# First attention tile scored in two halves, three weight conversions moved in VectorE's order, some high parts on VectorE

## The chip, the cores and the metric

The kernel runs on one core of a Trainium2 chip. The metric is the device time of one execution in microseconds; several runs are taken and their median is given. Engines are named as the profile names them: PE is the matrix engine (TensorE), PEld its weight loads, DVE is VectorE, ACT is ScalarE, POOL is GpSimd and SP is SyncE, which here only issues transfers. Every engine works through its own instructions in the order in which the program issues them, and waits where an instruction needs something that is not there yet.

## The reference

Two stages. First, attention over 8 batches, 8 heads, 576 positions and 64 channels a head, with a causal window of 64 positions. Then a mixer over the attention's output, first across positions (tokens), then across channels, each with a residual or sum:

```
scores = q @ k.T / 8;  masked unless 0 <= pos_q - pos_k < 64
attn   = softmax(scores);   x = attn @ v                 # x: (8, 576, 512)
h = relu(x.T @ w_tok1) @ w_tok2;  u = x + h.T            # 576 -> 256 -> 576
out = u + relu(u @ w_ch1) @ w_ch2                        # 512 -> 1536 -> 512
```

q, k and v are 32-bit floats; the four weight matrices arrive as 64-bit floats, and the kernel turns them into 32-bit floats itself by integer operations.

## The kernel before, in words

Products of the mixer are made exact enough by splitting each factor into a rounded high part (`hi`) and the rest (`lo`) and adding three matmuls, hi by hi, hi by lo and lo by hi. So almost every tile goes through a rounding copy (mostly ScalarE) and a subtraction (VectorE or GpSimd); `split` (L107) does both.

The attention and the token mixer run in one loop (L483) over i from -1 to 36. There are 36 attention tiles: `tile_blocks` (L81) gives each two blocks of 64 queries, nine tiles for a pair of batches. The loop is pipelined by hand; a pass i holds, in the order in which instructions are issued:

- loads of v for tile i+2, q for tile i+3, and k for a batch (L484 to 489), all on SyncE's queue;
- `pt_transpose` (L308) of tile i: PE transposes eight blocks of exponentials (pp), ScalarE copies them out (pt, L314);
- `softmax` (L285) of tile i+1: eight VectorE operations (L297) that add the mask, scale and take the minimum of the negated scores, one for each head;
- `recip` (L329) of the sums of tile i; in passes before `N_START` = 7 its first step is on GpSimd (L333), later on VectorE (L335);
- `job_finish` (L253) of a converted weight: high part on ScalarE, low part on GpSimd or, for the token mixer's second matrix, on VectorE (both L109 and L112);
- `split_x` (L346) of an attended tile that is ready: xhi on ScalarE, xlo on GpSimd (L109, L112);
- `softmax_exp` (L300) of tile i+1: eight exponentials on ScalarE (L305), four for u = 0 and four for u = 1, where u is the odd or even head of a pair;
- `tok1` (L443) of an earlier tile: six matmuls into h (L372); at the last tile of a batch `finish_h` (L379) takes the two high parts hhi from h on ScalarE (L383), and `finish_h_low` (L386) the low parts hlo on VectorE (L392);
- `av` (L319): 32 matmul records of attended values, xp (L324), and `norm` (L339), VectorE's multiplication by the reciprocal sums (L341);
- `qk` (L269) of tile i+2: 32 matmul records of scores, s (L282);
- `tok2` pieces (L400): transposes and matmuls into up (L413, L420), copied to u by ScalarE (L425); `run_pieces` is called after the first exponentials and again at the end of a pass. The bank that up lies in is single, so a piece waits until the copy of the piece before it is done.

Weight conversions are jobs, at most one a pass, by the hand-written table `JOBS` (L43); jobs 0 to 3 belong to w_tok1, jobs 4 to 6 to w_tok2. A job has a first half, `job_convert_a` (VectorE, L204, L206, L207), a second half, `job_convert_b` (VectorE, L216, L218, L219, then GpSimd's addition w, L221), and `job_finish` in the next pass. Before pass 7 both halves stand behind `norm`; from pass 7 on the first half stands ahead of `tok1` and the second behind the exponentials and ahead of `av` and `norm`. Passes 7 and 8 convert jobs 5 and 6.

`qk(0)` puts its scores into two banks of the tag "s" (u = 0 and 1, four heads each), `qk(1)` into the two of the tag "h", later tiles into "s". Banks of one tag are reused in turn, and the reuse waits for the last reader. xp lies in the single bank "av".

Ahead of the loop (L462 to 473) SyncE's queue issues the first loads in this order: q of tile 0; the first two blocks of k of the two groups that tile 0 needs, in one transfer; q of tile 1; the rest of these groups' blocks; v of tile 0; the first raw weights; the last k blocks; q of tile 2; raw weights; v of tile 1. Five matmuls on zeros (L480, L481, ten records) stand ahead of `qk(0)`.

The second stage, the channel mixer (from L562), follows; the change does not touch it.

Of the kernel before, what the change touches and what calls it, by code (L numbers as in the profile page):

```python
# [10 lines left out]
F32 = mybir.dt.float32  # L11
# [4 lines left out]
AF = mybir.ActivationFunctionType  # L16
# [28 lines left out]

TOK1_FROM, TOK1_SLOW, TOK2_FROM = 2, 7, 9

N_START = 7

NX = 4  # L50
NCHUNK = TOK // CHUNK
# [39 lines left out]
def mixer_kernel(ctx: ExitStack, tc: tile.TileContext, qh, kh, vh, wt1, wt2, wc1, wc2, out):  # L91
# [39 lines left out]
    with ExitStack() as actx:  # L131
# [16 lines left out]
        def load_q(i):  # L148
            qr = pq.tile([P, H // 2, 2, BLK], F32, name=f"q{i}", tag="q", bufs=5)
            nc.sync.dma_start(qr, qh[i])  # L150
            loaded[i] = [qr, None]
# [94 lines left out]
        def job_convert_b():  # L246
            if to_convert_b:
                n, part = to_convert_b.pop(0)
                to_finish.append((n, to_f32_b(*part)))
# [19 lines left out]
        def qk(i):  # L269

            qt = loaded[i][0]
            s = []
            for u in range(2):

                s.append(ps.tile([P, 4, P], F32, name=f"s{i}_{u}", tag="h" if i == 1 else "s", bufs=2))
                s_ps[i, u] = s[u]
            for j in range(4):
                for u in range(2):
                    r = slice(u * BLK, (u + 1) * BLK)
                    for half, (b, n) in enumerate(tile_blocks(i)):  # L280
                        so = s[u][half * BLK:(half + 1) * BLK, j].rearrange("p (n c) -> p n c", n=2)
                        nc.tensor.matmul(so, qt[r, j, half], kbs[b][r, n:n + 2, j],  # L282
                                         start=True, stop=True)

        def softmax(i, u):  # L285
            if u == 0:
                st[i] = (pa.tile([P, H], F32, name=f"nm{i}", tag="nm", bufs=3),
                         pa.tile([P, H], F32, name=f"sum{i}", tag="sum", bufs=3))
            nm, sm = st[i]
            mk = mask[1 if tile_blocks(i)[0][1] == 0 else 0]  # L290
            e = pa.tile([P, 4, P], F32, name=f"e{i}_{u}", tag="e", bufs=4)
            e_sb[i, u] = e

            s = s_ps.pop((i, u))
            for h in range(4):
                g = 2 * h + u
                nc.vector.tensor_tensor_reduce(out=e[:, h], in0=s[:, h], in1=mk, scale=-scale, scalar=MAX_F32,  # L297
                                               op0=ALU.add, op1=ALU.min, accum_out=nm[:, g:g + 1])

        def softmax_exp(i, u):  # L300
            e = e_sb[i, u]
            nm, sm = st[i]
            for h in range(4):
                g = 2 * h + u
                nc.scalar.activation(e[:, h], e[:, h], AF.Exp, bias=nm[:, g:g + 1], scale=-1.0,  # L305
                                     accum_out=sm[:, g:g + 1])

# [71 lines left out]
        def finish_h(b):  # L379
            h_hi[b] = []  # L380
            for tt in range(NTT):
                hi = pa.tile([P, C], F32R, name=f"hhi{b}_{tt}", tag=f"hhi{tt}", bufs=2)
                nc.scalar.activation(hi, h_ps[b][tt], AF.Relu)  # L383
                h_hi[b].append(hi)

        def finish_h_low():  # L386
# [71 lines left out]
        def run_pieces(k):  # L458
            for _ in range(min(k, len(pieces))):
                tok2(*pieces.pop(0))  # L460

        load_k(0)  # L462
        load_q(0)
        k0, kh0 = (x[:, :8].rearrange("p (g n) j c -> p g n (j c)", g=2) for x in (kbs[0], kh[0]))
        nc.sync.dma_start(k0[:, :, :2], kh0[:, :, :2])
        load_q(1)
        nc.sync.dma_start(k0[:, :, 2:], kh0[:, :, 2:])
        load_v(0)
        job_load()
        nc.sync.dma_start(kbs[0][:, 8:], kh[0, :, 8:])  # L470
# [12 lines left out]
        for i in range(-1, NT + 1):  # L483
            if 0 <= i and i + 2 < NT:  # L484
                load_v(i + 2)
            if 3 <= i + 3 < NT:
                load_q(i + 3)
            if i + 4 < NT:
                load_k(i + 4)
            store_u()  # L490
            n_jobs = JOBS[i]
            if i == NT - 1:
                up_tags += [("s", 2), ("pt", 2)]
            have = len(pieces)
            n_pieces = PIECES.get(i, (1, 1) if i >= TOK2_FROM else (0, 0))
            pts = []
            if 0 <= i < NT:
                pts.append(pt_transpose(i, 0))
                if i < NT - 1:
                    pts.append(pt_transpose(i, 1))  # L500
            if i + 1 < NT:
                softmax(i + 1, 0)
            if i + 1 < NT:
                softmax(i + 1, 1)
            if 0 <= i < NT:
                ri = recip(i)
            if i >= N_START:
                while to_finish:
                    job_finish()
            for n in tok1_plan.get(i + 1, ()):  # L510
                last_use = n - NX + ((n - NX) % TPP == 4)
                if n < i and last_use not in tok1_plan.get(i, ()):
                    split_x(n)
            while to_finish:
                job_finish()
            if i + 1 < NT:
                softmax_exp(i + 1, 0)
            run_pieces(min(have, n_pieces[0]))
            have = min(have, len(pieces))
            if i >= N_START:  # L520
                for _ in range(n_jobs):
                    job_convert_a()
            if i == NT - 1:
                pts.append(pt_transpose(i, 1))
            if i < N_START:
                softmax_exp(i + 1, 1)
            for n in tok1_plan.get(i, ()):
                tok1(n)
            if N_START <= i < NT - 1:
                softmax_exp(i + 1, 1)  # L530
            if i >= N_START:
                for _ in range(n_jobs):
                    job_convert_b()
            if 0 <= i < NT:
                norm(i, av(i, pts), ri)
            finish_h_low()
            if i < N_START:
                for _ in range(n_jobs):
                    job_convert_a()
                    job_convert_b()  # L540
            if i + 2 < NT:
                qk(i + 2)
            for n in tok1_plan.get(i + 1, ()):
                if n not in xhl:
                    split_x(n)
            run_pieces(min(have, n_pieces[1]))
            while to_load and len(to_convert) < 2 and i < NT - 2:
                job_load()
            if i == NT - 1:
                while to_convert or to_convert_b or to_finish:  # L550
                    job_convert_a()
                    job_convert_b()
                    job_finish()
                qctx.close()
                pu = uctx.enter_context(tc.tile_pool(name="pu", bufs=1, side="right", reuse_waits="tile"))
                ul = {0: load_u(0, pu)}
# [537 lines left out]
```

## Time and profile before

| what | value |
|---|---|
| median of 3 runs | 800.99 us (800.95 to 801.45) |
| the profiled execution | 801.79 us, its span 799.8 us |
| PE busy | 787.4 us, 98% of the span |
| VectorE busy | 570.2 us, 71% |
| ScalarE busy | 388.3 us, 49% |
| GpSimd busy | 262.5 us, 33% |
| granted PE clock | 0.999 |
| traffic | 180.59 MB, mean 226 GB/s |

Times in the profile count from the start of the span. A row of a timeline gives the start, the duration, the engine, the line, the operation, the output and inputs by the program's names, and in brackets how long the engine had been idle before and what ended that. Rows that follow one another may be merged, with their count at the end.

### The profile page before, as it was taken

Reading aid. Unit: us, or ns where it says so; the run is one execution under the profiler, and the core shown is the slowest. Engines: PE = TensorE matmul, PEld = TensorE weight load, DVE = VectorE, ACT = ScalarE, POOL = GpSimd, SP = SyncE. Lnnn points to the kernel's source line nnn. Section 1 sums busy time; section 2 is a strip of 40 time slices with the busy share of each in tenths; the row PEclk is TensorE's granted clock in tenths of the full one; section 3 lists DMA queues with packets and bytes.
Section 4 is the critical chain, followed back from the end, with each engine's and each line's share of the span. In section 5 each row is a group of like instructions: output and inputs, shape, how many; then the busy total and the mean of one; then the engine's idle time right before and its main releaser. Section 6 shows DMA issues by size and latency. Waiting matters only on the chain.

```text
span 799.8 us, 15811 instructions
## 1 busy us (share of the span) xinstructions
PE 787.4 (98%) x5749; PEld 654.8 (82%) x5749; DVE 570.2 (71%) x1533; ACT 388.3 (49%) x1124; POOL 262.5 (33%) x237
## 2 busy tenths in 40 slices
PE   8999999999999999999999999999999999999997
PEld 6667888888889888888888888888888888888886
DVE  5978789589582795777788474757766667656576
ACT  6999889889874441323334141326332244324040
POOL 3634545445330000000000050549732638723140
PEclk9999999999999999999999999999999999999999
DMA  9856779668635537877655775765985756955543
GB/s 352 282 179 229 235 251 304 223 217 308 218 113 170 197 103 216 257 225 235 207 164 193 275 289 184 258 236 203 294 320 201 288 187 207 349 209 191 201 159 105
DMA packets 86828, 180.59 MB, mean 226 GB/s; under 512 B 8800, under 2 KB 51808, under 8 KB 84832
## 3 DMA queue, kind: packets, MB, share of 16 engines
q1 hardware_dynamic: 84640, 177.76, 64.4%
q10 hardware_dynamic: 2112, 1.84, 0.7%
q8 instruction: 45, 0.74, 0.4%
q14 instruction: 31, 0.25, 0.1%
HBM read 137.69 MB, written 41.88 MB: 225 GB/s over the span
## 4 chain that ended last, share of the span: by engine, by line
PE 93%; ACT 3%; DVE 3%; POOL 1%; issue 1%; DVEq 0%; ACTq 0%
PE op L969 22%; PE gp L913 21%; PE op L643 12%; PE gp L635 12%; PE up L420 6%; PE h L372 6%; PE xp L324 4%; PE s L282 3%; PE pp L312 3%; PE up L413 3%; ACT e L305 2%; DVE e L297 1%; PE idle L481 1%; DVE x L341 1%; POOL xlo L112 0%
## 5 line engine op out<-in xcount | busy, mean ns | idle before, releaser
L913 PE MATMUL gp<-m,w1hi 128*128 128x512 f32 x504 | 155.1, 389 | 0.0
L112 POOL TENSOR_TENSOR m7lo<-t3g,m7hi 128x512 fp32r<-128x512 f32 x18 | 23.4, 1300 | 359.4 <-ACT m7hi L109 359.4
L305 ACT ACTIVATE e<-e,nm 128x128 f32<-128x128 f32 x288 | 112.3, 398 | 5.7 <-DVE nm L297 5.7
L913 PEld LDWEIGHTS gp<-m,w1hi 128*128 128x128 f32 x504 | 94.6, 188 | 19.6
L913 PE MATMUL gp<-m,w1lo 128*128 128x512 f32 x252 | 98.0, 389 | 0.0
L958 DVE TENSOR_TENSOR uf<-op,uf 128x512 f32<-128x512 f32 (+1 forms) x91 | 61.9, 684 | 39.5 <-PE op L969 31.7
L297 DVE CUSTOM_DVE_ANT_0 e<-s,mask 128x128 f32<-128x128 f32 x288 | 63.5, 286 | 12.5 <-PE s L282 12.4
L112 POOL TENSOR_TENSOR xlo<-x,xhi 128x512 fp32r<-128x512 f32 x32 | 41.2, 1289 | 46.3 <-ACT xhi L109 46.0
L305 ACT ACTIVATION_READ_ACCUMULATOR e<-e,nm 128x1 f32 x288 | 56.3, 196 | 0.0
L635 PE MATMUL gp<-ulo,w1hi 128*128 128x512 f32 x144 | 56.0, 389 | 0.0
L635 PE MATMUL gp<-uhi,w1hi 128*128 128x512 f32 x144 | 56.0, 389 | 0.0
L635 PE MATMUL gp<-uhi,w1lo 128*128 128x512 f32 x144 | 56.0, 389 | 0.0
L913 PEld LDWEIGHTS gp<-m,w1lo 128*128 128x128 f32 x252 | 47.3, 188 | 9.9
L916 ACT COPY x<-gp 128x512 f32<-128x512 f32 x18 | 10.6, 588 | 80.8 <-PE gp L913 80.8
L643 PE MATMUL op<-glo,w2hi 128*128 128x512 f32 x128 | 49.8, 389 | 0.0
L643 PE MATMUL op<-ghi,w2hi 128*128 128x512 f32 x128 | 49.8, 389 | 0.0
L643 PE MATMUL op<-ghi,w2lo 128*128 128x512 f32 x128 | 49.8, 389 | 0.0
L221 POOL TENSOR_TENSOR w<-r,c 128x384 f32<-128x384 f32 (+1 forms) x28 | 27.6, 985 | 59.8 <-DVE r L219 57.8
L324 PEld LDWEIGHTS xp<-v,pt 128*64 128x64 f32 x1152 | 36.6, 138 | 12.9 <-ACT e L305 10.1
L341 DVE TENSOR_TENSOR x<-xp,ri 128x512 f32<-128x512 f32 x36 | 24.9, 691 | 30.1 <-PE xp L324 29.5
L312 PE MATMUL pp<-ident,e 128*128 128x128 f32 x288 | 44.2, 281 | 1.3
L420 PE MATMUL up<-t2hi,hhi 128*128 128x320 f32 (+1 forms) x128 | 43.0, 336 | 0.0
(204 smaller groups left out, 2040.3 us busy)
## 6 DMA issues: line engine op xcount, KB each, us to landing
v<-vh SPq DMA_DIRECT2D x36, 512.0 KB, 4.0
w1hi<-w1s SPq DMA_DIRECT2D x18, 896.0 KB, 5.1
w1lo<-w1s SPq DMA_DIRECT2D x18, 896.0 KB, 7.1
w1hi<-w2s SPq DMA_DIRECT2D x18, 896.0 KB, 4.6
w1lo<-w2s SPq DMA_DIRECT2D x18, 896.0 KB, 6.4
raw<-wc SPq DMA_DIRECT2D x32, 384.0 KB, 4.3
q<-qh SPq DMA_DIRECT2D x36, 256.0 KB, 4.8
k<-kh SPq DMA_DIRECT2D x7, 1280.0 KB, 8.0
```

The costliest lines, as they stand in the source:

```text
L112: eng_lo.tensor_sub(lo, src, hi.bitcast(F32))
L297: nc.vector.tensor_tensor_reduce(out=e[:, h], in0=s[:, h], in1=mk, scale=-scale, scalar=MAX_F32, op0=ALU.add, op1=ALU.min, accum_out=nm[:, ...
L305: nc.scalar.activation(e[:, h], e[:, h], AF.Exp, bias=nm[:, g:g + 1], scale=-1.0, accum_out=sm[:, g:g + 1])
L312: nc.tensor.transpose(pp[:, h], e[:, h], ident)
L324: nc.tensor.matmul(xp[half * BLK:(half + 1) * BLK, h], pts[h % 2][:, h // 2, half * BLK:(half + 1) * BLK], vt[:, half, h], start=True, sto ...
L372: nc.tensor.matmul(h_ps[b][tt], w[:, o + tt * P:o + (tt + 1) * P], x, start=first and n == 0, stop=last and n == len(combos) - 1)
L420: nc.tensor.matmul(up[:, :n], hx[:, cs], w[:, tt * S + s0:tt * S + s0 + n], start=False, stop=(k == 6), skip_group_check=True)
L635: nc.tensor.matmul(gp, w[:, w1_at(ft, ct)], x[:, ct], start=(k == 0), stop=(k == 3 * NCT - 1))
L643: nc.tensor.matmul(op, w[:, ct, ft], x[:, cols], start=(first and k == 0), stop=(last and k == 3 * len(gs) - 1), skip_group_check=not (fir ...
L913: nc.tensor.matmul(b[INTO[m]], w[:, at], c[:, h, t], start=(k < 4 and z == y == 0), stop=(z == 1 and y == 2), skip_group_check=True)
L958: eng.tensor_add(x, y, x)
L969: nc.tensor.matmul(bank[:, cols], w[:, o:o + P], x[:, cols], start=(i == 0 and y == 0 and m in ("m1", "m6", "m7", "m5")), stop=(i == 1 and ...
```

## The change

Four edits.

1. Loads and scores of tile 0. q of tile 0 and the first two k blocks are loaded in two halves of the head pairs j (0 and 1, then 2 and 3); each half's k goes in two transfers, one on SyncE's queue and one on ScalarE's. The rest of k's blocks, which tile 1 needs, goes on ScalarE's queue too. The scores of tile 0 go into four banks, two of "s" for j below 2 and two of "h" for the rest, so that the first four heads are a tile of their own for VectorE and ScalarE; `softmax` and `softmax_exp` of tile 0 take u = 0 and 1 of the first two j, then of the other two. The scores of tile 1 go into "up" and "av".
2. In pass 0, the first half of the conversion stands ahead of `av` and `norm`.
3. In passes 7 and 8, the second half of the conversion stands at the end of the pass, behind `norm`, `qk` and `split_x`, and ahead of the pieces.
4. For even batches (0, 2, 4, 6), the second of the two high parts of h is taken by VectorE (a maximum with zero) and not by ScalarE.

```
--- before.py
+++ after.py
@@ -45,7 +45,7 @@
 
 TOK1_FROM, TOK1_SLOW, TOK2_FROM = 2, 7, 9
 
-N_START = 7
+N_START, N_SPLIT = 7, 9
 
 NX = 4
 NCHUNK = TOK // CHUNK
@@ -269,39 +269,43 @@
         def qk(i):
 
             qt = loaded[i][0]
-            s = []
-            for u in range(2):
-
-                s.append(ps.tile([P, 4, P], F32, name=f"s{i}_{u}", tag="h" if i == 1 else "s", bufs=2))
-                s_ps[i, u] = s[u]
+            tags = (("up", 1), ("av", 1)) if i == 1 else (("s", 2), ("s", 2))
+            s = [ps.tile([P, 4, P], F32, name=f"s{i}_{u}", tag=tag, bufs=bufs) for u, (tag, bufs) in enumerate(tags)]
+
+            s_ps[i] = s + (s if i else [ps.tile([P, 4, P], F32, name=f"s{i}_{u + 2}", tag="h", bufs=2)
+                                        for u in range(2)])
             for j in range(4):
                 for u in range(2):
                     r = slice(u * BLK, (u + 1) * BLK)
                     for half, (b, n) in enumerate(tile_blocks(i)):
-                        so = s[u][half * BLK:(half + 1) * BLK, j].rearrange("p (n c) -> p n c", n=2)
+                        so = s_ps[i][j // 2 * 2 + u][half * BLK:(half + 1) * BLK, j].rearrange("p (n c) -> p n c", n=2)
                         nc.tensor.matmul(so, qt[r, j, half], kbs[b][r, n:n + 2, j],
                                          start=True, stop=True)
 
-        def softmax(i, u):
-            if u == 0:
+        def heads(i, part):
+
+            if i == 0:
+                return [(u, h) for u in range(2) for h in range(2 * part, 2 * part + 2)]
+            return [(part, h) for h in range(4)]
+
+        def softmax(i, part):
+            if part == 0:
                 st[i] = (pa.tile([P, H], F32, name=f"nm{i}", tag="nm", bufs=3),
                          pa.tile([P, H], F32, name=f"sum{i}", tag="sum", bufs=3))
             nm, sm = st[i]
             mk = mask[1 if tile_blocks(i)[0][1] == 0 else 0]
-            e = pa.tile([P, 4, P], F32, name=f"e{i}_{u}", tag="e", bufs=4)
-            e_sb[i, u] = e
-
-            s = s_ps.pop((i, u))
-            for h in range(4):
+            for u, h in heads(i, part):
+                if (i, u) not in e_sb:
+                    e_sb[i, u] = pa.tile([P, 4, P], F32, name=f"e{i}_{u}", tag="e", bufs=4)
                 g = 2 * h + u
-                nc.vector.tensor_tensor_reduce(out=e[:, h], in0=s[:, h], in1=mk, scale=-scale, scalar=MAX_F32,
-                                               op0=ALU.add, op1=ALU.min, accum_out=nm[:, g:g + 1])
-
-        def softmax_exp(i, u):
-            e = e_sb[i, u]
+                nc.vector.tensor_tensor_reduce(out=e_sb[i, u][:, h], in0=s_ps[i][h // 2 * 2 + u][:, h], in1=mk,
+                                               scale=-scale, scalar=MAX_F32, op0=ALU.add, op1=ALU.min,
+                                               accum_out=nm[:, g:g + 1])
+
+        def softmax_exp(i, part):
             nm, sm = st[i]
-            for h in range(4):
-                g = 2 * h + u
+            for u, h in heads(i, part):
+                e, g = e_sb[i, u], 2 * h + u
                 nc.scalar.activation(e[:, h], e[:, h], AF.Exp, bias=nm[:, g:g + 1], scale=-1.0,
                                      accum_out=sm[:, g:g + 1])
 
@@ -380,7 +384,10 @@
             h_hi[b] = []
             for tt in range(NTT):
                 hi = pa.tile([P, C], F32R, name=f"hhi{b}_{tt}", tag=f"hhi{tt}", bufs=2)
-                nc.scalar.activation(hi, h_ps[b][tt], AF.Relu)
+                if b % 2 == 0 and tt == 1:
+                    nc.vector.tensor_scalar(out=hi, in0=h_ps[b][tt], scalar1=0.0, scalar2=None, op0=ALU.max)
+                else:
+                    nc.scalar.activation(hi, h_ps[b][tt], AF.Relu)
                 h_hi[b].append(hi)
 
         def finish_h_low():
@@ -460,11 +467,17 @@
                 tok2(*pieces.pop(0))
 
         load_k(0)
-        load_q(0)
+        q0 = pq.tile([P, H // 2, 2, BLK], F32, name="q0", tag="q", bufs=5)
+        loaded[0] = [q0, None]
         k0, kh0 = (x[:, :8].rearrange("p (g n) j c -> p g n (j c)", g=2) for x in (kbs[0], kh[0]))
-        nc.sync.dma_start(k0[:, :, :2], kh0[:, :, :2])
+        for part in range(2):
+            js = slice(part * 2, part * 2 + 2)
+            nc.sync.dma_start(q0[:, js], qh[0, :, js])
+            js = slice(part * 2 * BLK, (part + 1) * 2 * BLK)
+            for g, eng in enumerate((nc.sync, nc.scalar)):
+                eng.dma_start(k0[:, g, :2, js], kh0[:, g, :2, js])
         load_q(1)
-        nc.sync.dma_start(k0[:, :, 2:], kh0[:, :, 2:])
+        nc.scalar.dma_start(k0[:, :, 2:], kh0[:, :, 2:])
         load_v(0)
         job_load()
         nc.sync.dma_start(kbs[0][:, 8:], kh[0, :, 8:])
@@ -528,21 +541,27 @@
                 tok1(n)
             if N_START <= i < NT - 1:
                 softmax_exp(i + 1, 1)
-            if i >= N_START:
+            if i >= N_SPLIT:
                 for _ in range(n_jobs):
                     job_convert_b()
+            if i == 0:
+                job_convert_a()
             if 0 <= i < NT:
                 norm(i, av(i, pts), ri)
             finish_h_low()
             if i < N_START:
                 for _ in range(n_jobs):
-                    job_convert_a()
+                    if i > 0:
+                        job_convert_a()
                     job_convert_b()
             if i + 2 < NT:
                 qk(i + 2)
             for n in tok1_plan.get(i + 1, ()):
                 if n not in xhl:
                     split_x(n)
+            if N_START <= i < N_SPLIT:
+                for _ in range(n_jobs):
+                    job_convert_b()
             run_pieces(min(have, n_pieces[1]))
             while to_load and len(to_convert) < 2 and i < NT - 2:
                 job_load()
```

## The prediction

> **What bounds the kernel now.** I read a table of busy times by stage, then what the matrix engine (PE) waits for, then the order of time of the first 70 us, engine by engine.
>
> ```profile
> 0.00:65.00 65.00, 57.86 (x804) 42.20 (x805) 49.26 (x246) 53.81 (x209) 30.05 (x50) 1.00 0.77 276
> 65.00:240.00 175.00, 174.22 (x2440) 153.40 (x2437) 139.28 (x616) 152.77 (x570) 77.02 (x66) 1.00 0.69 230
> 240.00:799.80 559.80, 555.28 (x2515) 459.22 (x2513) 381.63 (x671) 181.76 (x346) 155.45 (x121) 1.00 0.63 219
> ```
> ```profile
> PE h L372 <- POOL xlo L112: 1.4, 2, 0.9
> PE s L282 <- DMA k<-kh: 1.3, 1, 1.3
> ...
> PE h L372 <- DVE hlo L392: 1.0, 1, 1.0
> PE up L413 <- ACT u L425: 0.7, 2, 0.4
> ...
> PE h L372 <- ACT xhi L109: 0.3, 1, 0.3
> ```
>
> The columns of the first fence are the stretch, its length, then busy PE, weight loads, VectorE (DVE), ScalarE (ACT), GpSimd (POOL), clock, DMA. PE is without work for 65.00 - 57.86 = 7.1 us in the first 65 us, for 0.8 us up to 240, and for 4.5 us in the feed-forward stage, which the change does not touch. From about 65 us PE runs without gaps, so what counts is when it gets there, plus the 0.7 us that it waits for copies of u. The prize is about 8 us at the very most; most of it is a start-up that the change shortens only a little.
>
> The sum is made against the profiled execution, 801.79 us with its span of 799.8 us; it lies 0.80 us above the median, 800.99 us, and I take the differences over unchanged. Under 0.2% (1.6 us) a time cannot be told from no change here.
>
> **First tile in two halves.**
>
> ```profile
> 1.17 4.64 PE L481 MATMUL idle<-zero 128*128 128x256 f32 x10 [1.17 <-DVE zero L161]
> ...
> 2.13 0.43 SPq L467 DMA_DIRECT2D k<-kh  x1
> ...
> 5.73 1.47 PE L282 MATMUL s<-k,q 64*64 64x128 f32 x32
> ...
> 7.70 0.40 ACT L305 ACTIVATE e<-e,nm 128x128 f32<-128x128 f32 x1 [5.70 <-DVE nm L297]
> ...
> 8.51 1.10 PE L282 MATMUL s<-k,q 64*64 64x128 f32 x32 [1.30 <-DMA k<-kh]
> ...
> 11.41 1.22 PE L324 MATMUL xp<-v,pt 128*64 128x64 f32 x32
> ...
> 12.68 0.69 DVE L341 TENSOR_TENSOR x<-xp,ri 128x512 f32<-128x512 f32 x1 [1.05 <-PE xp L324]
> 13.29 0.32 DVE L204 TENSOR_SCALAR c<-raw 128x320 int32<-128x320 int32 x1
> ...
> 14.36 0.49 DVE L216 SCALAR_TENSOR_TENSOR c<-raw,c 128x320 int32<-128x320 int32 x1
> ...
> 15.83 0.87 POOL L221 TENSOR_TENSOR w<-r,c 128x320 f32<-128x320 f32 x1 [4.61 <-DVE r L219]
> ...
> 16.73 0.46 ACT L109 CAST t1hi<-w 128x320 fp32r<-128x320 f32 x1 [0.23 <-POOL w L221]
> ```
> ```profile
> L282 PE MATMUL s<-k,q x128: 269/269/473, 5.7 to 18.4; 64*64 64x128 f32 x128
> ```
>
> The first scores cannot start earlier: the warm-up matmuls run to 1.17 + 4.64 = 5.81 and the scores follow without a gap, so data that comes sooner gains nothing. What is gained is that VectorE may start on half of the scores. A tile's 32 records take 1.10 us with a last one of 0.27, so the second sixteen stand for (1.10 - 0.27) / 2, about 0.42. The first exponential moves from 7.70 to 7.27, and ScalarE, busy 53.81 us in these 65 and so with hardly a pause from there on, moves with it. Bounds: 0 if the first half lands too late, 0.73 if the halves were equal parts of the 1.47. I take 0.43, from the warm rows, because the second half runs warm.
>
> SyncE's queue now issues two q and two k quarters, each about 0.43, before q of tile 1, which goes out some 0.9 later; v and the raw weights behind it some 0.4 later. ScalarE's queue issues three k pieces while ScalarE has nothing else to do (idle until 7.70). The scores of tile 1 move from the two "h" banks into "up" and "av", so the first xp matmul, also in "av", must now wait until VectorE has read them. If k's rest lands as today (scores from 8.51 to 9.61, then eight maxima, done before 11.5), xp starts at 11.5 in place of 11.41, its norm at 12.8, and the conversion below still meets its date. So that costs nothing; if it lands a microsecond sooner, nothing is gained either, as ScalarE sets the pace.
>
> ```profile
> k<-kh SPq DMA_DIRECT2D x1, 512.0 KB, 6.2
> ```
>
> K's rest, issued at 2.13, landed 6.2 later, at 8.3, one of several transfers on one queue; no row shows two loading queues side by side. [...]
>
> **Conversion of tile 0 ahead of its norm.**
>
> ```profile
> raw<-wt SPq DMA_DIRECT2D x1, 320.0 KB, 7.4
> ```
>
> VectorE waits 1.05 us for xp before the norm. The three moved operations take 14.36 - 13.29 = 1.07; the raw weights, two transfers behind k's rest and so issued at about 3.1, land 7.4 later, at 10.5, now perhaps 10.9; xp ends, 0.43 earlier, at 12.2. So they fit into the wait. The norm is at 12.25, the second half of the conversion at 12.86, and GpSimd's w, 15.83 - 14.36 = 1.47 behind it, at 14.3, ready at 15.2. ScalarE reaches t1hi at 16.73 - 0.23 (the wait) - 0.10 - 0.43 = 15.97 and no longer waits; the 0.10 is what operations that don't wait overlap the one before (12.68 + 0.69 against 13.29 is 0.08). So the exponentials of tile 2 gain 0.43 + 0.33 = 0.76.
>
> ```profile
> 21.99 1.15 PE L324 MATMUL xp<-v,pt 128*64 128x64 f32 x32
> ...
> 23.19 0.69 DVE L341 TENSOR_TENSOR x<-xp,ri 128x512 f32<-128x512 f32 x1
> ...
> 28.70 0.69 DVE L341 TENSOR_TENSOR x<-xp,ri 128x512 f32<-128x512 f32 x1
> ```
>
> VectorE itself gains more, 1.5, but loses it at tile 2: its norm at 23.19 follows an xp that ended at 23.14, and that xp comes only 0.76 earlier. From there VectorE has no pause (no idle time stands at these norms, which are 5.51 apart), so 0.76 is what stays through tiles 3 to 6.
>
> **Conversions of tiles 7 and 8 behind the norm.** This is the dear part.
>
> ```profile
> 52.94 1.15 PE L324 MATMUL xp<-v,pt 128*64 128x64 f32 x32
> ```
> ```profile
> 53.51 0.56 DVE L219 SCALAR_TENSOR_TENSOR r<-raw,r 128x384 f32<-128x384 uint32 x1
> 54.14 0.69 DVE L341 TENSOR_TENSOR x<-xp,ri 128x512 f32<-128x512 f32 x1
> ```
> ```profile
> 54.14 1.00 POOL L221 TENSOR_TENSOR w<-r,c 128x384 f32<-128x384 f32 x1 [3.63 <-DVE r L219]
> 55.56 1.28 POOL L112 TENSOR_TENSOR xlo<-x,xhi 128x512 fp32r<-128x512 f32 x1 [0.42 <-ACT xhi L109]
> ...
> 61.80 1.28 POOL L112 TENSOR_TENSOR xlo<-x,xhi 128x512 fp32r<-128x512 f32 x1 [0.25 <-ACT xhi L109]
> ```
> ```profile
> 56.71 0.53 ACT L109 CAST t2hi<-w 128x384 fp32r<-128x384 f32 x1
> ...
> 61.11 0.62 ACT L109 CAST xhi<-x 128x512 fp32r<-128x512 f32 x1 [0.78 <-DVE x L341]
> ...
> 62.59 0.52 ACT L109 CAST t2hi<-w 128x384 fp32r<-128x384 f32 x1
> ...
> 67.05 0.62 ACT L109 CAST xhi<-x 128x512 fp32r<-128x512 f32 x1
> 67.78 0.37 ACT L425 COPY u<-up 128x256 f32<-128x256 f32 x1
> ```
> ```profile
> 68.46 0.38 PE L413 MATMUL up<-ident,x 128*128 128x128 f32 x2
> ```
>
> At tile 7 the norm starts when xp ends (52.94 + 1.15 = 54.09), and the conversion before it has ended then too (54.07). Moving it frees nothing. But it moves w behind xlo on GpSimd, and t2hi, which needs w, stands ahead of all the next exponentials on ScalarE. Step by step, with the start gain: norm 7 at 53.38; xlo 1.42 later, 54.80 to 56.08; then w, 1.00, to 57.08 (VectorE's part is done by 55.6); t2hi at 57.11, where today it is at 56.71 with no wait. Queued behind the moved steps on VectorE are the maxima of tile 9, some 1.1 later than today but done by 57.3, before the exponentials at 57.5 need the last. From t2hi to the end of the eight exponentials is 61.11 - 0.78 - 56.71 = 3.62, so xhi of tile 8 starts at 60.73. (Its norm no longer waits for the conversion; with t2lo and three conversion steps ahead of it, it is done at about 60.0 and isn't the later one.) Then GpSimd does xlo, 61.80 - 61.11 = 0.69 behind xhi, to 62.70, then w to 63.70; t2hi at 63.73 against 62.59. ScalarE's work from t2hi to the next xhi has no pause and takes 67.05 - 62.59 = 4.46: xhi at 68.19, the copy of u 0.52 behind it (0.62 less the overlap), done at 69.08, and the second up, which waits for that bank, at 69.1 against 68.46. So a gain of 0.76 has become a loss of 0.65: the part costs 1.41. Bounds: 0, if ScalarE could make the delay up elsewhere; 2.0, both w in full behind xlo. PE has no pause after 68.46 in which to recover.
>
> **Half of the inner high parts on VectorE.**
>
> ```profile
> 45.49 0.69 DVE L341 TENSOR_TENSOR x<-xp,ri 128x512 f32<-128x512 f32 x1 [1.57 <-PE xp L324]
> ```
> ```profile
> 101.71 0.44 PE L413 MATMUL up<-ident,x 128*128 128x128 f32 x2 [0.45 <-ACT u L425]
> ```
> ```profile
> 162.76 0.44 PE L413 MATMUL up<-ident,x 128*128 128x128 f32 x2 [0.28 <-ACT u L425]
> ```
>
> Four operations of PE's result, 128x512, go to VectorE, about 0.69 each by the norm's row, the nearest that reads PE's banks. Queued behind each is the norm of that tile, which waits for xp; PE does xp after the h that the new operation waits for, so the norm comes no later as long as 0.69 fits in the 1.15 of xp. In the first of them VectorE had idled 1.57. ScalarE is free of the operation, about 0.5. At the first it gains nothing (the low part waits for the other half, which stays). At the second and third, PE waited 0.45 and 0.28 for a copy of u that stood behind both high parts: 0.73 in all goes away, bounds 0 and 0.73.
>
> **Sum.** -0.76 + 1.41 - 0.73 = -0.08 us: 801.7 for the profiled execution, 800.9 for the median.
>
> **The rivals.** *The moved conversions pay* (faster). The norm of tile 8 does start about a microsecond behind its xp, and PE waits 0.9 + 0.3 for tile 8 and the other 0.5 for tile 7. If the exponentials are not held by t2hi, the 1.41 goes and about 1.0 of those waits with it: -0.76 - 1.0 - 0.73 = -2.5, 798.5. For it: the waits are real. Against: ScalarE's order puts t2hi first. I give 0.12.
>
> *The two queues collide* (slower). K's rest is now issued on the second queue beside the second half's pieces on the first, and can hold that half back. That decides from about 7.1, when VectorE runs out of the first four heads (an estimate: four maxima behind the first). If the half lands at 9.0, exponentials 5 to 8 start about 1.2 later (from first score to first exponential is 1.97 for a whole tile), at 10.2 in place of 7.70 + 4 x 0.39 = 9.26; the start loses 0.9 - 0.33 = 0.6 and the total is 0.6 + 1.41 - 0.73 = +1.3: 802.3. For it: 0.5 MB more in flight. Against: on its own queue the half's piece goes first. I give 0.12. [...]
>
> *ScalarE's relief buys nothing* (the waits for u stay, since the copy is held by something else): +0.6, 801.6. I give 0.1.
>
> **How the numbers follow.** 0.66 for the sum as it stands. Its own ends: the start between -0.35 and -1.1, the conversions between 0.6 and 2.0, the relief 0 to 0.73, which together rarely move it by more than 1 us. The range, 799.6 to 802.5, takes in the slower rivals and leaves out the faster one. Faster by over 1.6 us needs the first rival, 0.12; slower by over 1.6 us needs the collision and the dear end of the conversions together, 0.07; within it, 0.81.
>
> **What would show it.** Right: first exponential near 7.27, t1hi without a wait near 15.97; t2hi waiting for GpSimd's w at tiles 8 and 9 (about 57.1 and 63.7); xlo ahead of w on GpSimd; the second up waiting for a copy of u near 69; no such wait at 101 and 162. Wrong: the first up piece and the second both earlier than now, a second half of the first tile that PE waits for, or a PE that idles in new places past 70 us.

## The result, and the profile after

The changed kernel takes 805.36 us, median of 6 runs (803.77 to 807.72); the kernel before, beside it, 801.07 (6 runs, 800.84 to 802.11). The ratio is 1.0051, 95% interval 1.0035 to 1.0068: slower by about 4.3 us, outside the range. The profiled execution of after is 805.72 us with a span of 803.7.

The table by stage of the kernel after, columns as before (length, then busy PE, weight loads, VectorE, ScalarE, GpSimd, clock, DMA share, GB/s):

```profile
0.00:65.00 65.00, 55.77 (x784) 41.53 (x785) 50.20 (x245) 51.23 (x198) 29.75 (x50) 0.99 0.76 270
65.00:240.00 175.00, 174.99 (x2450) 154.16 (x2448) 140.85 (x622) 152.83 (x575) 75.90 (x66) 0.99 0.69 231
240.00:803.70 563.70, 557.15 (x2521) 459.93 (x2518) 387.11 (x671) 182.38 (x348) 155.84 (x122) 1.00 0.63 218
```

PE is idle for 9.2 us of the first 65 (before 7.1), hardly at all up to 240 (before 0.8), and for 6.6 behind that (before 4.5), in a stage that the change does not touch. What it waits for, all of it in the first 72 us (times in us: in total, how often, the longest):

```profile
PE s L282 <- DMA q<-qh: 2.0, 2, 1.1
PE s L282 <- DMA k<-kh: 1.7, 1, 1.7
PE h L376 <- POOL xlo L112: 1.4, 2, 0.9
...
PE h L376 <- DVE hlo L399: 1.0, 1, 1.0
PE xp L328 <- ACT pt L318: 0.7, 1, 0.7
```

The first two rows are loads that come late, the others results of other engines. The order of time in five places follows; line numbers are those of the changed file, up to 19 higher than before.

**Start.**

```profile
5.73 0.92 PE L282 MATMUL s<-k,q 64*64 64x128 f32 x16
7.15 0.40 ACT L309 ACTIVATE e<-e,nm 128x128 f32<-128x128 f32 x1 [3.62 <-DVE nm L301]
8.40 1.70 PE L282 MATMUL s<-k,q 64*64 64x128 f32 x48 [1.75 <-DMA k<-kh]
9.43 0.40 ACT L309 ACTIVATE e<-e,nm 128x128 f32<-128x128 f32 x1 [0.63 <-DVE nm L301]
...
18.03 1.22 PE L282 MATMUL s<-k,q 64*64 64x128 f32 x32 [1.11 <-DMA q<-qh]
```

The first exponential comes at 7.15, 0.55 earlier than before. But the second half of the scores waits 1.75 us for its data, the fifth exponential is at 9.43 where 8.7 was due, and tile 3's q is late as well.

**Conversions.**

```profile
54.25 0.69 DVE L345 TENSOR_TENSOR x<-xp,ri 128x512 f32<-128x512 f32 x1 [1.64 <-PE xp L328]
...
55.68 1.27 POOL L112 TENSOR_TENSOR xlo<-x,xhi 128x512 fp32r<-128x512 f32 x1 [5.53 <-ACT xhi L109]
55.84 1.52 DVE L219 SCALAR_TENSOR_TENSOR r<-raw,r 128x384 f32<-128x384 uint32 x1
57.44 1.02 POOL L221 TENSOR_TENSOR w<-r,c 128x384 f32<-128x384 f32 x1 [0.49 <-DVE r L219]
58.49 0.51 ACT L109 CAST t2hi<-w 128x384 fp32r<-128x384 f32 x1 [1.55 <-POOL w L221]
...
64.00 1.00 POOL L221 TENSOR_TENSOR w<-r,c 128x384 f32<-128x384 f32 x1
65.04 0.51 ACT L109 CAST t2hi<-w 128x384 fp32r<-128x384 f32 x1 [1.47 <-POOL w L221]
...
70.94 0.38 PE L420 MATMUL up<-ident,x 128*128 128x128 f32 x2
```

The start gave nothing: tile 7's norm is at 54.25 (before 54.14), so the delay against the kernel before is 0.11 there. "Delay" below always means this: how much later the same operation stands than in the kernel before. From there to the second up, 2.37 us are lost (70.94 against 68.46, less 0.11), at the two places that the prediction named.

**Clock.** Two stretches around the second t2hi, columns as in the table by stage (the clock is the third number from the end):

```profile
60.92:64.33 3.41, 2.13 (x8) 0.99 (x7) 3.34 (x19) 2.65 (x10) 1.64 (x2) 1.00 0.86 306
64.33:67.75 3.42, 3.42 (x31) 2.48 (x32) 1.47 (x7) 2.71 (x11) 0.67 (x1) 0.50 0.75 296
```

For 3.41 us PE gets half its clock, directly behind a stretch of the same length in which it was busy for 2.13, 1.4 of that with transposes. In the profile of the kernel before, the granted clock falls to 0.5 at the very end of the span alone, at 798.43 us.

**High parts.** The places of the two old waits for u:

```profile
103.70 0.44 PE L420 MATMUL up<-ident,x 128*128 128x128 f32 x2
...
164.28 0.39 PE L420 MATMUL up<-ident,x 128*128 128x128 f32 x2
```

Neither waits any more; the delay falls from 2.48 to 1.99 and 1.52.

**Last stage.** The kernel before, then the one after:

```profile
649.93 0.68 DVE L870 SCALAR_TENSOR_TENSOR m3lo<-gp,m3hi 128x512 fp32r<-128x512 f32 x1
650.82 0.69 DVE L870 SCALAR_TENSOR_TENSOR t3g<-gp,g 128x512 f32<-128x512 f32 x1 [0.21 <-ACT g L929]
...
667.53 3.08 POOL L794 TENSOR_TENSOR m<-t,m 128x512 fp32r<-128x512 f32 x2
668.76 0.69 DVE L958 TENSOR_TENSOR uf<-u,uf 128x512 f32<-128x512 f32 x1
```
```profile
651.00 0.68 DVE L889 SCALAR_TENSOR_TENSOR m3lo<-gp,m3hi 128x512 fp32r<-128x512 f32 x1
652.26 0.69 DVE L889 SCALAR_TENSOR_TENSOR t3g<-gp,g 128x512 f32<-128x512 f32 x1 [0.58 <-ACT g L948]
...
668.75 2.53 POOL L813 TENSOR_TENSOR m<-t,m 128x512 fp32r<-128x512 f32 x2
669.83 6.99 DVE L977 TENSOR_TENSOR uf<-u,uf 128x512 f32<-128x512 f32 x1
671.25 2.52 POOL L977 TENSOR_TENSOR uf<-u,uf 128x512 f32<-128x512 f32 x2
673.74 2.53 POOL L813 TENSOR_TENSOR m<-r,m 128x512 fp32r<-128x512 f32 x2
...
679.27 0.50 PE L988 MATMUL op<-m2hi,w1hi 128*128 128x512 f32 x1 [1.42 <-DVE u L977]
```

At 651 the delay is 1.07, so the high parts have given 1.41 in all. Then one addition of VectorE takes 6.99 us instead of 0.69, while GpSimd works without a pause; PE waits behind it, and the delay grows to 3.6. The span has 0.35 more of clean-up behind the last matmul, as all kernels with the halves have. So the profile's account is 0.11 (start) + 2.37 (conversions and clock) - 1.41 (high parts) + 2.51 (the held addition) + 0.35 = 3.93, the 3.9 of the span.

So four accounts are to be explained: a start that gained nothing, conversions at 2.4, a halved clock, and a held addition far behind the change.

### The profile page after: what moved, and what is told of

Same layout as the page of the kernel before. It is cut to its first block, busy times and chain, and to the rows that moved or that the text cites. A ratio compares the mean times of both kernels' runs of the same rounds, so it can differ in the third digit from the quotient of the medians.

```text
span 803.7 us, 15813 instructions
## 1 busy us (share of the span) xinstructions
PE 787.9 (98%) x5749; PEld 655.6 (82%) x5749; DVE 578.2 (72%) x1537; ACT 386.4 (48%) x1120; POOL 261.5 (33%) x237
## 4 chain that ended last, share of the span: by engine, by line
PE 89%; DMA 3%; POOL 2%; ACT 2%; DVE 2%; issue 1%; SPq 0%; DVEq 0%; POOLq 0%; ACTq 0%
PE gp L932 20%; PE op L988 19%; PE gp L654 12%; PE op L662 12%; PE up L427 6%; PE h L376 6%; PE xp L328 4%; PE s L282 4%; PE pp L316 3%; PE up L420 3%; POOL m L813 2%; ACT e L309 1%; DMA q<-qh 1%; DMA k<-kh 1%; DMA w1lo<-w1s 1%
## 5 line engine op out<-in xcount | busy, mean ns | idle before, releaser
L282 PE MATMUL s<-k,q 64*64 64x128 f32 x1152 | 41.1, 277 | 3.8 <-DMA q<-qh 2.0
L328 PE MATMUL xp<-v,pt 128*64 128x64 f32 x1152 | 42.2, 227 | 0.8 <-ACT pt L318 0.7
```

The lines of the kernel that those rows point to most:

```text
L328: nc.tensor.matmul(xp[half * BLK:(half + 1) * BLK, h], pts[h % 2][:, h // 2, half * BLK:(half + 1) * BLK], vt[:, half, h], start=True, sto ...
```

## The experiments

Each kernel was run beside the kernel before, whose median was 801.39 for the runs of the first part below, 801.34 for the next four (k's rest on SyncE's queue, the idle matmuls, the two with sums on VectorE), 801.47 for the last kernel of "The held addition" and the last of "What remains", and 801.58 for the others. Differences are against the one beside. My first theory: the conversions are the loss, the first tile's loads collide, the high parts gain, and the held addition is an accident of small shifts.

### Each part by itself

The conversions alone, on the kernel before:

```
-            if i >= N_START:
+            if i >= N_SPLIT:
...
+            if N_START <= i < N_SPLIT:
+                for _ in range(n_jobs):
+                    job_convert_b()
```

N_SPLIT is 9; the lines at the end stand behind `split_x`.

> The kernel before with the conversions of tiles 7 and 8 alone moved behind the norm. Theory (these conversions are the loss around 60 us, and the halved clock there follows from PE's waits for xlo behind the late w): t2hi waits about 1.5 for w at tiles 8 and 9, and in the profile the granted clock falls to 0.5 for about 3.4 us near 62 to 68 us; second up +2 to +3 against the kernel before, total 803.0 to 804.5. Rival 1 (the halved clock has nothing to do with these waits): both waits of about 1.5, no 0.5 before the end of the span, second up +1.0 to +1.6, total 802.0 to 802.8. Rival 2 (the loss around 60 us came from the start): no loss, 801.1.

803.49 (8 runs, 802.65 to 804.86) against 801.39; ratio 1.0026 [1.0017, 1.0036]. The profile:

```profile
55.33 0.69 DVE L341 TENSOR_TENSOR x<-xp,ri 128x512 f32<-128x512 f32 x1 [1.66 <-PE xp L324]
...
59.57 0.51 ACT L109 CAST t2hi<-w 128x384 fp32r<-128x384 f32 x1 [1.55 <-POOL w L221]
...
66.11 0.51 ACT L109 CAST t2hi<-w 128x384 fp32r<-128x384 f32 x1 [1.46 <-POOL w L221]
...
71.50 0.44 PE L413 MATMUL up<-ident,x 128*128 128x128 f32 x2 [0.45 <-ACT u L425]
```

The clock stayed at 1.00 around these rows, and the same waits delay the second up by 3.04 (71.50 against 68.46), of which 1.19 were there at tile 7's norm already (55.33 against 54.14), from a halved clock at 8.9 to 12.3 us: in this very run the start, which this kernel does not change, lost 1.2. So the conversions cost 1.9 without the clock's help, and the 0.5 that is left of the 2.37 in after is put down to its halved clock at 64 us. Rival 1 is right that the clock is a matter of its own, but not on the price; the total lies in the theory's range without the halved clock that the theory counted on.

The high parts alone (`if b % 2 == 0 and tt == 1:` on VectorE):

> The kernel before with half of the four inner high parts alone on VectorE. Theory (this part worked, and more than forecast): PE's waits at 101 and 162 us gone and a third gain near 221, together -1.3, total 799.7. Rival 1 (the sum of the prediction): -0.73, 800.3. Rival 2 (the late operation of VectorE that took 6.99 us is set off by the stage before arriving about a microsecond off its old time): the gain of 1.3 is there at 240 us and lost in the last 140 us, total 800.5 to 802.5 and spread over more than a microsecond between runs.

800.62 (11 runs, 799.89 to 801.27); ratio 0.9990 [0.9981, 0.9998]. The gain is there. In the profile it is 1.4 at 240 us (the delay goes from -0.35 to -1.75), but 0.7 of it is gone by 605: 0.36 go at 472 us and 0.17 at 561, by a pause of VectorE that "The held addition" comes to. The first of these places (in the kernel before, the wait is 0.73):

```profile
472.63 0.69 DVE L873 SCALAR_TENSOR_TENSOR t4g<-gp,t2g 128x512 f32<-128x512 f32 x1 [1.09 <-ACT m2hi L889]
```

The first tile in halves and the conversion of tile 0 ahead, without the other two parts:

> The kernel before with the first tile in halves and the conversion of tile 0 ahead of its norm, without the other two parts. Theory (the loads of the two halves and of k's rest collide): first exponential near 7.2, then PE waits about 1.7 for the second half of tile 0, tile 5 on time as before within 0.2; no halved clock near 65; total 801.1, within 0.3. Rival 1 (the sum of the prediction): tile 3 on 0.76 earlier, 800.3. Rival 2 (the start itself brings the loss around 60 us): second up +1 or more, total 802 or more.

803.52 (7 runs, 802.57 to 804.51); ratio 1.0027 [1.0016, 1.0037]. None of the three: the start by itself costs 2.1. Its profile in two stretches of 3.41 us:

```profile
4.86:8.27 3.41, 1.14 (x19) 0.56 (x17) 0.93 (x8) 1.65 (x8) 0.65 (x3) 1.00 0.95 335
8.27:11.68 3.41, 3.23 (x50) 2.93 (x51) 1.19 (x11) 1.65 (x8) 0.00 (x0) 0.50 1.04 403
```

The second half comes at 8.46 here too, PE is busy for only 1.14 of 3.41 us, and the next 3.41 run at half clock. All seven runs have a mean clock of .998 or less; of the 23 of the kernel before beside them one has (in a later group 6 of 27, so it is not spared either). The profile of after had by luck been spared this at the start: its clock rose at 6.31, and the stretch of 3.41 us from there had 1.7 busy.

The changed kernel without its move of the conversions (`N_SPLIT = 7`):

> The changed kernel with the conversions of tiles 7 and 8 put back where they were. Theory (they bring the loss at 60 us, the rest gains about 1.3): second up within 0.3 of the kernel before, no halved clock near 65, total 799.5 to 800.0 where VectorE's late operation isn't held up, 802 to 802.5 in runs where it is. Rival (the loss comes from the first tile's halves, or from the parts together): still over 803.5.

804.69 (7 runs, 801.83 to 805.54); ratio 1.0034 [1.0022, 1.0046]. The rival: 3.3 of the 4.3 us are still there without the moved conversions. The profile has the halved clock at the start (6.8 us long), and the addition held for 6.99 us again, which neither the start alone nor the high parts alone had. My first theory falls; two accounts had to be settled.

### The start: collision and clock

K's rest on SyncE's queue, behind q of tile 1, the rest as in the run of the start alone:

```
-        nc.scalar.dma_start(k0[:, :, 2:], kh0[:, :, 2:])
+        nc.sync.dma_start(k0[:, :, 2:], kh0[:, :, 2:])
```

> The run of the start alone, with k's rest issued on SyncE's queue behind q of tile 1 instead of on ScalarE's. Theory (k's rest on the second queue takes its share from the second half of tile 0): the second half lands by about 7.3, PE waits under 0.8 for it in place of 1.75, fewer runs with a halved clock, total 800.5 to 801.5. Rival (the second half takes until 8.3 whatever is issued beside it): the wait stays over 1.4, total 803 to 804.

802.00 (11 runs, 801.32 to 803.08) against 801.34; ratio 1.0010 [1.0000, 1.0019]: 1.5 better than with k's rest on ScalarE's queue, and still no gain.

```profile
4.93 0.67 PE L282 MATMUL s<-k,q 64*64 64x128 f32 x16
6.05 0.67 PE L282 MATMUL s<-k,q 64*64 64x128 f32 x16 [0.46 <-DMA k<-kh]
8.18 1.10 PE L282 MATMUL s<-k,q 64*64 64x128 f32 x32 [1.46 <-DMA k<-kh]
...
17.48 1.83 PE L282 MATMUL s<-k,q 64*64 64x128 f32 x30 [1.55 <-DMA q<-qh]
```

The second half now comes 0.5 behind the first: the collision was real, and it is the one that the prediction held as a rival. But what the first tile gains, PE waits for at tile 3 (17.48), for q. From 3 to 15 us the DMA engines have a busy share of 1.02 in the kernels before and after. So the account that fits is that the loads, not the order of the scores, set the pace of the start; no run with fewer or smaller loads tested it.

The run of the start alone, with three idle matmuls on zeros between the two halves (added work):

> The kernel with the first tile in halves and the conversion of tile 0 ahead (the run of the start alone), and three idle matmuls more, on zeros, between the first tile's two halves, where PE waits for data. Theory (PE's emptier first microseconds let the clock fall to half in the window behind them, and that is what the start costs): no 0.5 in the clock before the end, mean clock .999 in most runs, total 801.0 to 801.8 against 803.5 without them, though it adds work. Rival 1 (the halved clock isn't set by PE's idle time there): still dips, 803 to 804. Rival 2 (the start costs through late data alone): no dips, but still over 803.

802.87 (11 runs, 802.18 to 803.53); ratio 1.0018 [1.0010, 1.0027]. Between the theories: 0.6 better than without the idle work, mean clocks .998 to 1.000 where they were .994 to .998, but still 1.5 over the kernel before. The gap costs through the clock, and something is left that it does not explain. The profiled run, the fastest of the eleven (802.18), does not show it: PE waits for q at tiles 3 and 4 (1.14 and 0.93 us), yet the delay at 460 us is 0.02, and only the clean-up at the end is longer.

### The held addition

First attempt, on the changed kernel: GpSimd's two sums beside it put on VectorE (`eng2 = nc.vector`).

> The changed kernel with GpSimd's two last sums of the sixth product (of all pairs of chunks but the last) on VectorE. Theory (VectorE's sum is held for 6.99 us while GpSimd works without a pause, in most runs of the changed kernel): no operation of VectorE over 2 us near 670, PE without waits there, total about 2.5 below the changed kernel in the runs that had it: median 802.8 to 803.5, and less spread. Rival (VectorE gets too full with the two sums and delays PE itself, or the 6.99 happened in the profiled run alone): 805 to 806.

806.61 (5 runs, 805.36 to 807.57); ratio 1.0063 [1.0051, 1.0076]: slower still. No addition is held for 7 us, though several of VectorE's beside GpSimd take 1.6 to 1.8 in place of 0.69; and the sums delay VectorE's own work for PE twice, which the waits show:

```profile
PE gp L932 <- DVE x L941: 2.4, 2, 1.2
```

The same on the high parts alone:

> The kernel before with half of four inner high parts on VectorE and the same two sums on VectorE. Theory: the gain of the first (0.8 in the time, 1.7 in the profile at 240 us) comes through whole, 799.3 to 800.0. Rival (the sums on VectorE cost more than they save): 800.6 or more.

803.38 (10 runs, 802.98 to 804.25); ratio 1.0025 [1.0016, 1.0034], 2.8 over the high parts alone. Both expectations missed: the cure costs as much as the illness, and says nothing of its cause.

The cause showed when the two t3g rows above were compared: t3g waits 0.37 longer after its input g is done (0.58 against 0.21) with no other releaser. Counting VectorE's records, waits included, from the span's start (the first is number 0), it is number 1599 in both kernels that hold the addition; in the start alone, number 1599 is t2g, and that starts 0.41 behind the wait ahead of it, where 0.04 is usual; in the high parts alone it is a mere wait.

```profile
653.50 0.69 DVE L952 SCALAR_TENSOR_TENSOR t2g<-gp,t1g 128x512 f32<-128x512 f32 x1 [0.47 <-DVE t1g L886]
```

So the pause belongs to the count, not to the operation. Two tests move the count alone, by memsets of one column in idle VectorE time at the start:

```
         nc.vector.memset(zero, 0.0)
+        spare = pa.tile([P, 1], F32, name="spare")
+        for _ in range(3):
+            nc.vector.memset(spare, 0.0)
```

The kernel before with three of them:

> The kernel before with three tiny memsets of VectorE more at the same place, which put t3g at the 1599th record. Theory: t3g pauses 0.4 us, GpSimd's chain behind it is 0.4 late, VectorE's sum near 669 is held for about 7 us, and the kernel before loses 2 to 2.6 with nothing else changed: 803.3 to 804.0. Rival (the hold has another origin): no difference, 801.3.

803.89 (9 runs); ratio 1.0022 [1.0012, 1.0033]. Seven runs lie between 803.25 and 804.14, two at 801.13 and 801.21, nothing between. The profiled run is one of the two:

```profile
650.51 0.69 DVE L873 SCALAR_TENSOR_TENSOR t3g<-gp,g 128x512 f32<-128x512 f32 x1 [0.56 <-ACT g L932]
...
666.96 3.03 POOL L797 TENSOR_TENSOR m<-t,m 128x512 fp32r<-128x512 f32 x2
668.09 0.73 DVE L961 TENSOR_TENSOR uf<-u,uf 128x512 f32<-128x512 f32 x1
```

The pause is there, but the addition, which starts 1.13 behind GpSimd's pair, just slips in between GpSimd's two operations. After has 669.83 - 668.75 = 1.08 and is held, before has 1.23; but the changed kernel without its move of the conversions has 1.13 too and is held, so this is a close race, and the profiles give no limit. Three memsets of no use cost this kernel 2.3 us in most runs. Those runs have no profile; that they are the ones held fits the 2.7 between the two groups, near the 2.5 that the held addition cost after.

The changed kernel with one:

> The changed kernel with one tiny memset of VectorE more, right after the one for the warm-up, where VectorE is idle. Theory (VectorE pauses for 0.4 us at its 1599th record, whatever operation stands there; in the changed kernel that is t3g at 652 us, on which GpSimd's chain hangs, and GpSimd 0.4 late holds VectorE's sum for 6.99 us): one record more puts the pause on a wait, t3g starts on time, no operation over 2 us on VectorE near 670, no gain lost after 640 us; the shift against the kernel before at the end is within 0.3 of that at 640 us; total about 2.4 lower than the changed kernel, median 802.7 to 803.6. Rival (the 6.99 us come from something else, a race that one memset doesn't change): 805 to 806.

804.44 (5 runs, 802.67 to 804.64); ratio 1.0030 [1.0018, 1.0042]. In the profile t3g is on time, nothing is held, and nothing is lost from 640 us to the last matmul:

```profile
653.14 0.69 DVE L892 SCALAR_TENSOR_TENSOR t3g<-gp,g 128x512 f32<-128x512 f32 x1 [0.21 <-ACT g L951]
...
671.07 0.69 DVE L980 TENSOR_TENSOR uf<-u,uf 128x512 f32<-128x512 f32 x1
```

The runs fall in two groups: 802.67 and 802.80 with a mean clock of .999, three at 804.4 to 804.6 with .997. The median missed what I expected; in the profile, one of the slower three, the clock is halved from 9.3 to 12.7 us and tile 7's norm is 1.24 late (0.11 in after), so the start took back what the memset gave.

The high parts and tile 0's conversion ahead, nothing else of the change:

> The kernel before with half of four high parts on VectorE and with tile 0's conversion ahead of its norm, nothing else. By the sum of the prediction the conversion gains 0.33 as t1hi no longer waits for w: 800.3 against the 800.6 of the high parts alone. Rival (the loads of q for tiles 3 and 4 end later than the work that this brings forward, so nothing is gained): 800.6, and PE waits for q at tile 3 or 4.

802.77 (12 runs, 799.52 to 803.51); ratio 1.0011 [1.0003, 1.0020]: neither. Moving the conversion had also removed one wait from VectorE's list, so t3g was number 1599 once more:

```profile
648.63 0.69 DVE L876 SCALAR_TENSOR_TENSOR t3g<-gp,g 128x512 f32<-128x512 f32 x1 [0.56 <-ACT g L935]
...
665.10 2.57 POOL L800 TENSOR_TENSOR m<-t,m 128x512 fp32r<-128x512 f32 x2
666.21 7.00 DVE L964 TENSOR_TENSOR uf<-u,uf 128x512 f32<-128x512 f32 x1
```

With one memset more:

> High parts on VectorE and tile 0's conversion ahead of its norm, with one tiny memset of VectorE more at the start. Theory (the pause at the 1599th record stood at t3g in the run without the memset and cost its gain): no hold near 670 in nearly all runs, median 799.5 to 800.2, faster than the kernel before and than the high parts alone (800.6). Rival (the conversion ahead of the norm costs something itself): 801 or more.

800.54 (11 runs, 799.62 to 802.74) against 801.47; ratio 0.9988 [0.9979, 0.9997], against the kernel beside it 2.1 less by a memset, though 0.3 over the end of what I expected. It beats the kernel before by 0.9; the high parts alone did by 0.8, so the conversion ahead of the norm adds nothing that can be told.

### What remains

All three losses taken out of the changed kernel (conversions back, k's rest on SyncE, one memset):

> The changed kernel without what the theories call its three losses: conversions of tiles 7 and 8 back in place, k's rest on SyncE's queue, one tiny memset of VectorE more. Theory (the parts add up): 801.34 + 0.66 (first tile without the collision, as measured) - 0.8 (high parts) = 801.2, and no hold near 670. Rival 1 (the first tile in halves does gain once the other losses are gone): 800.0 to 800.5. Rival 2 (something else in the changed kernel costs as well): over 802.

802.43 (11 runs, 800.94 to 802.85); ratio 1.0008 [1.0000, 1.0017]. The five runs with a clock of .999 or 1.000 lie at 800.94 to 801.80, around the sum of the parts; the other six, at .998 or less, set the median. The halves gain nothing even so. The profile also loses 0.5 at records 1343 and 1471, as the high parts alone do.

The changed kernel with one memset and the idle matmuls between the halves:

> The changed kernel with one tiny memset of VectorE and with three idle matmuls between the two halves of tile 0. Theory (the runs at 804.5 of the changed kernel with the memset, clock .997, are those whose clock was halved behind PE's gap in the first tile; those at 802.7, clock .999, weren't): with the gap filled nearly all runs have a clock of .998 or more and take 802.3 to 803.3. Rival (the clock falls whatever PE does there): most runs still at 804 to 805.

803.60 (6 runs, 803.11 to 804.48); ratio 1.0029 [1.0018, 1.0041]. All clocks are .998 or .999 now, and against the kernel before the median is 0.7 better than without the idle work (+2.1 where it was +2.9). So the clock at the start does follow PE's gap; but the best two runs without the idle work are not reached, and the profile has a halved clock at 64.8 us, as after had at 64.3.

## Why the prediction was wrong, step by step

- **"What is gained is that VectorE may start on half of the scores", 0.43.** The first exponential did come earlier, by 0.55. But the step took for granted that the second half is there when the first is worked off; PE could start on it at 8.40 only. The rival for this was on record at 0.12, with the right place and nearly the right moment (9.0), and the runs bear it out: with k's rest behind q of tile 1 the half comes at 6.05, where it came at 8.46 with k's rest on ScalarE's queue. The rival too was short of the truth: also without the collision tile 3 waits 1.55 for its q, at a DMA share of 1.02.
- **Conversion of tile 0, 0.33.** t1hi waits no more, as forecast, and it is worth nothing measurable. In after, tile 3 then waits for q (1.11); in the two kernels with this move and without the halves PE waits for no q in the first 45 us, so there it stays open why nothing shows.
- **Conversions of tiles 7 and 8, 1.41.** Right in mechanism and in both places; mis-sized. "VectorE's part is done by 55.6" failed: L219 ran beside GpSimd's xlo and took 1.52 instead of 0.56 (the same in the run of the conversions alone), so w started 0.49 behind xlo. The part measured 1.9 by itself in the profile, 2.1 in the median.
- **High parts, 0.73.** Right, and short: 1.41 in the profile of after, with a third gain behind 165 us that no wait of PE showed. In the median of the part alone it is 0.8, after the two pauses named above.
- **"The feed-forward stage, which the change does not touch."** True of the code, and it is the step that failed most: the sum had no term for that stage, and in the profile of after it lost 2.5 us, by a pause of 0.41 us that the count of VectorE's records put on t3g.
- **The clock.** No term stood for it. It rises and falls in steps of 3.41 us: between its first rise and its last fall the stretches of one clock are 58.03, 3.41 and 733.87 us long in after, which is 17, 1 and 215 steps, and 791.89 in the kernel before, 232 steps. With PE's longer gap in the first tile (2.46 us in the start alone, 1.30 before) the mean clock was .994 to .998 in all seven runs, where 22 of the 23 runs of the kernel before had .999 or more. The clock fell behind stretches with 1.14 us (the start alone) and 2.13 us (after) of busy PE, and stayed at 1.00 behind one with 1.66 at the start of after. Of the 2.13, 1.4 were transposes; that these decide it is not borne out: the kernel with one memset and the idle matmuls lost its clock behind 2.24 us with 0.7 of transposes, and the start filled with idle matmuls kept it around 60 us behind 2.25 with 1.0 of them.

What stays open: how much work in a stretch keeps the clock (at the start busy shares of 0.33, 0.39 and 0.42 lost it, in the start alone, the changed kernel with one memset and the conversions alone, and 0.49 kept it in after; around 61 us 0.63 lost it in after and 0.66 in the kernel with one memset and the idle matmuls, and 0.66 kept it in the kernel before), and the 1.5 us that the filled start still costs in the median.

## What to carry to other kernels

Before a first tile is split to start sooner, look at the DMA share of those microseconds: at 1.02, an earlier start here only moved the wait to a later tile (1.55 us at tile 3), and with the gap in between PE's mean clock was .994 to .998 in all seven runs of the start alone. A step that was moved behind another on VectorE dragged what it feeds on other engines behind that engine's own next work: w started 0.49 us behind xlo, and t2hi waited 1.55 for it. And a few microseconds far behind an edit (2.5 here) may be a matter of the record of VectorE on which a pause of 0.4 falls: shift the count by a memset or two before believing that an edit costs them.

## What the runs showed of the hardware that was not expected

- VectorE's record 1599 starts 0.40 to 0.41 us behind the wait ahead of it, where 0.04 is usual, whether t3g stands there (after, the kernel before with three memsets, the high parts with tile 0's conversion ahead) or t2g (the start alone). The same pause of 0.40 shows at record 319 in before and after and at 1727 in after; the high parts alone lose their 0.36 and 0.17 at records 1343 and 1471. All are whole multiples of 128 records away from 1599, and in before and after it shows at such a place only where the record is an operation right behind a wait. What it is that pauses, no run shows.
- An addition of VectorE (uf from u and uf) was held for 6.99 us in after, from 669.83 to 676.82, while GpSimd did six operations of 1.25 us back to back, to 676.27. Held ones had started 1.08 to 1.13 us behind GpSimd's pair; one at 1.13 and those at 1.22 or more got through, in 0.69 to 0.73. By what the one holds the other, no run shows.
- PE's clock was halved for one step of 3.41 us, beginning at 8.27 us in the profile of the start alone, 8.90 in the conversions alone, 9.28 in the changed kernel with one memset, 64.33 in after and 64.8 in the kernel with one memset and the idle matmuls; in the changed kernel without its move of the conversions it was two steps, 6.8 us.
